# Two-kind attention, then a leaky-ReLU feed-forward layer: the start of the schedule laid out anew

## The chip, the cores and the metric

One core of a Trainium2 chip runs the whole program. Five engines share the work: TensorE (PE in the profile) multiplies matrices into PSUM, VectorE (DVE) and ScalarE (ACT) move and transform tiles, GpSimd (POOL) casts, sets constants and issues some of the transfers, SyncE (SP) issues most transfers. The metric is the device time of one execution in microseconds (us), the lower the better. Before the change the median of three runs was 291.47 us (291.08 to 293.45).

## The reference

Four batches, 8 heads, 768 positions, head size 64. Heads 0, 2 and 6 ("retrieval") attend causally to everything before them; the other five ("streaming") see the first 4 positions (the sinks) and a window of the last 64. The attention output, laid out as 3072 rows of 512, goes through two matrix products with a leaky ReLU between them.

```python
scores = scale * np.matmul(q, k.transpose(0, 1, 3, 2))
stream_keep = causal & (is_sink | in_win)
scores = np.where(mask[None, :, :, :], scores, -1000000000.0)
a = np.exp(scores - np.max(scores, axis=-1, keepdims=True))
a = a / (np.sum(a, axis=-1, keepdims=True) + 1e-09)
x = np.matmul(a, v)            # then rows (batch, position) by 512
h = x @ w_in                   # 512 -> 2048
g = np.maximum(0.01 * h, h)
out = g @ w_out                # 2048 -> 512
```

## The kernel before

The 3072 rows are cut into eight **chunks** of 384 rows, two per batch (even chunks are a batch's first half, `c == 0`; odd ones, `c == 1`, also attend to the first half). For each chunk n the work is:

- **load** (L68): q, k and v come from memory as three fp32 tiles named `f`, of which the pool holds 4. For chunks 0 and 1, k and q are one transfer each (chunk 0's are halves); a later tile is three transfers of 256 KB. Chunks 0 and 1 are issued on SP, chunk 2 on POOL, the others on SP.
- **casts** to bf16 by POOL (`cast_qk`, `cast_v`, L183 to L192): k to `kb`, q to `qb`, v to `va`. Chunk 0 is cast by DVE, ACT and POOL together.
- **v_shift** (L194): the streaming heads read v at an offset of 64 rows; two transfers issued on ACT copy `va` to `vb`. For chunk 0 this is done with matmuls by a shift matrix (`v_shift_pe`, L201).
- **prep_pair** (L215): for a pair of heads, 3 transposes of `kb` and 3 of `qb` on PE, then three moves out of PSUM, two into `kt` and one into `qt`. The PSUM tag `pt` has a single bank, so the next pair's transposes wait until the three moves are done. Four pairs a chunk.
- **attention** (class `Attention`): units of a head. A unit has a score part (`qk`: matmuls into a PSUM bank `psS`, an exponential on ACT into `at` or `ats`, a mask on DVE) and a value part (`do_av`: matmuls by `va`/`vb` into `po`). A retrieval head has 2 units in an even chunk and 5 in an odd one, a streaming head 1. The sink unit (L269) serves all streaming heads. `finish` normalizes a pair of heads on DVE into `xs`; `x_t` transposes `xs` on PE and ACT moves it to `xt`. `slots` (L379) lays the units out so that a unit's values come two slots after its scores.
- **product 1** (`in_slots`, L415): 16 ticks of 4 matmuls, each followed by the leaky ReLU on ACT into `g`.
- **product 2** (`out_slots`, L427): three PSUM results of 16 matmuls each, cut into 16 slots of 2 to 4 matmuls; `py` has one bank; DVE copies a result to `o` and SP stores it.

The whole order is written out by hand: `run` emits lists of slots, `merge(a, b)` spreads list b evenly between the entries of list a, and every engine executes its instructions in the order emitted. From chunk 2 on a loop does the same for each n: product 1 of chunk n, product 2 of chunk n - 1 and the attention of chunk n + 1 (with the preps of chunk n + 2 between) are merged.

The stretch ahead of this loop, the **ramp**, is laid out by itself (L471 to L541): chunk 0's first four heads are scored, its v is cast and shifted, their values begin, and then the second half of its q and k is cast; weights are issued on POOL (`w_in` four times, then `w_out` four times, then chunk 2). Then come chunk 1's attention merged with half of product 1 of chunk 0, the rest of product 1 of chunks 0 and 1 alone, product 2 of chunk 0 alone, nine slots of product 2 of chunk 1 merged with the preps and the attention of chunk 2, and the preps of chunk 3 alone. The loop starts with seven slots of product 2 of chunk 1 left.

Of the kernel before, what the change touches and what calls it, by code (L numbers as in the profile page):

```python
# [17 lines left out]
CH = 384  # L18
# [3 lines left out]
def kernel(  # L22
# [72 lines left out]
    load(0, "k", 0)  # L95
    load(0, "q", 0)
    load(0, "v")
    load(0, "k", 1)
    load(0, "q", 1)
# [18 lines left out]
    ats = [bf(f"ats{i}", 3, 4, 64) for i in range(4)]  # L118
# [7 lines left out]
    def zeros(i):  # L126
        eng = nc.vector if i == 0 else nc.gpsimd
        eng.memset(kt[i][64:128, :, 0, :], 0.0)
        eng.memset(kt[i][0:64, :, 1, :], 0.0)
        nc.gpsimd.memset(va[i][:, :, :, D], 1.0)  # L130
        nc.gpsimd.memset(ksink[i][:], 0.0)
        nc.gpsimd.memset(vs[i][:, 0, :], 0.0)

    def constants():
# [10 lines left out]
        for a in ats:  # L145
            nc.gpsimd.memset(a[:, :, 1:3, :], 0.0)
# [47 lines left out]
    def v_shift(n):  # L194
# [3 lines left out]
        nc.scalar.dma_start(out=vb[i][0:64, lo:hi], in_=va[i][64:128, lo:hi])  # L198
        nc.scalar.dma_start(out=vb[i][64:128, lo:hi], in_=va[i][0:64, lo + 1 : hi + 1])

    def v_shift_pe():  # L201

        for t in range(2):
# [8 lines left out]
            nc.scalar.activation(out=vb[0][:, t, 1:8:2, :], in_=src, func=ACTF.Copy)  # L212
            nc.scalar.activation(out=vb[0][:, t, 4, :], in_=p[:, 4 * w : 5 * w], func=ACTF.Copy)
# [32 lines left out]
    class Attention:  # L246
        def __init__(self, n, score_tags=("psS",)):
# [5 lines left out]
            self.tags = score_tags  # L253
            self.sc = 0
# [3 lines left out]
        def av(self, p, hh, qi, lhsT, rhs):  # L258
            first = p not in self.po
            if first:  # L260
                self.po[p] = bank("po", [128, 3, 2, D + 1], FP32)
# [7 lines left out]
        def sink(self):  # L269
            i, c = self.i, self.c  # L270
            if c == 0:
                for h in range(H):
                    if not IS_RETR[h]:
# [3 lines left out]
                s = self.score()  # L277
                nc.tensor.matmul(s[:, 0 : 7 * (D + 1)], lhsT=e_sink[:], rhs=va[i][:, 0, 1:H, :],
                                 start=True, stop=True)
                nc.vector.tensor_tensor(  # L280
                    vs[i][:, 1:H, :], s[:, 0 : 7 * (D + 1)].rearrange("p (h d) -> p h d", h=7),
                    m_sink[:, 1:H, :], op=ALU.mult)
# [8 lines left out]
        def retr(self, h):  # L291
# [5 lines left out]
            for grp in groups:  # L297
                box = {}

                def qk(grp=grp, box=box):  # L300
                    s = self.score()
                    a = rot.tile([128, CH], BF16, name="at", tag="at", bufs=5)
# [76 lines left out]
        def slots(self, extra=()):  # L379
# [7 lines left out]
            last = {p: max([j for j, u in enumerate(units) if u[2] == p]) for p in range(4)}  # L387
            last[0] = max(last[0], [j for j, u in enumerate(units) if u[1] is None][0])
# [83 lines left out]
    ktb, qtb = cast_tile("k", 0), cast_tile("q", 0)  # L472

    def cast_half(half):
        hs = slice(4 * half, 4 * half + 4)
        nc.vector.tensor_copy(ktb[:, :, hs], qk_src("k", 0)[:, :, hs])
        nc.scalar.activation(out=qtb[:, :, hs], in_=qk_src("q", 0)[:, :, hs], func=ACTF.Copy)

    a0 = Attention(0, ("psS", "ph"))
    cast_half(0)  # L480
    prep_pair(0, 0, "pt", "vva")
    prep_pair(0, 1, "py", "aav")
    u = [a0.units[h] for h in range(H)]
    first = u[0] + u[2]
    run([x[0] for x in first])
    nc.gpsimd.tensor_copy(va[0][:, 0, :, 0:D], v_src(0)[:, 0])
    nc.vector.tensor_copy(va[0][:, 1, :, 0:D], v_src(0)[:, 1])
    nc.gpsimd.tensor_copy(va[0][:, 2, :, 0:D], v_src(0)[:, 2])
    late_constants()
    run([x[0] for x in u[1] + u[3]])  # L490
    sink_mask()
    cast_qk(1)
# [100 lines left out]
```

## Time and profile before

| what | value |
|---|---|
| median of three runs | 291.47 us (291.08 to 293.45) |
| the profiled execution: its own time | 291.4 us |
| its span, first to last instruction | 289.7 us |
| mean granted clock of PE | 0.971 |
| busy PE, ACT, DVE, POOL | 250.7, 142.7, 114.9, 67.3 us |
| moved by DMA | 32.11 MB (27.26 MB read from memory, 6.29 MB written) |

The page shows busy times of the engines, a picture of the span in 40 slices, the DMA queues, the chain of work that ended last and the costliest groups. In a row of a timeline stand the start, the length, the engine, the line, the operation and, in brackets, how long the engine had been idle and what released it. In a row of stretches stand its bounds, its length and, for each engine, busy time and count, then the granted PE clock (1.00 is full), the share of the 16 DMA engines that was busy and GB/s. Matmuls are pipelined: the step from one start to the next is shorter than the duration that a row shows; the chain rows give the steps.

### The profile page before, as it was taken

The page shows a single profiled execution, that of the slowest core. Times are in us where ns is not written, and L with a number is a line of the kernel's source. Part 1 is how long each engine was busy: PE and PEld are TensorE (multiplying, and loading weights), DVE is VectorE, ACT ScalarE, POOL GpSimd, SP SyncE. Part 2 cuts the span into 40 slices and gives each one's busy share as a digit, 9 for nine tenths or more (in the row PEclk, how much of TensorE's full clock was granted, in tenths as well). Part 3 has the DMA queues.
Part 4 walks back from the last instruction along what each step waited for, and adds up shares of the span by engine and source line. Part 5 has one row for each costly group of instructions (what it writes and reads, how often), then busy time and mean ns, then how long its engine had stood idle before and what let it go on. Part 6 is the DMA issues. An engine that isn't in the chain of part 4 may idle for free.

```text
span 289.7 us, 5396 instructions
## 1 busy us (share of the span) xinstructions
PE 250.7 (87%) x2164; PEld 153.4 (53%) x2164; DVE 114.9 (40%) x320; ACT 142.7 (49%) x311; POOL 67.3 (23%) x113
## 2 busy tenths in 40 slices
PE   0658469899976756999989999999999999999995
PEld 0447336555434433666556656666566566655544
DVE  6757324200046744255455523554455124311012
ACT  2644747667002511776545466654554657643310
POOL 7579326920004243520042004300000000000000
PEclk9999978999999985999999999999999999999999
DMA  8999999500239799910793079502000301010022
GB/s 188 252 214 194 188 226 239 121 0 0 75 113 224 152 222 204 221 47 3 158 207 85 27 147 195 116 36 75 36 7 33 94 37 38 0 38 36 36 74 73
DMA packets 66921, 32.11 MB, mean 111 GB/s; under 512 B 54032, under 2 KB 62480, under 8 KB 66896
## 3 DMA queue, kind: packets, MB, share of 16 engines
q1 hardware_dynamic: 60832, 22.81, 35.6%
q0 software_dynamic: 4944, 6.55, 12.6%
q10 hardware_dynamic: 1120, 2.40, 3.6%
q8 instruction: 17, 0.28, 0.4%
q14 instruction: 8, 0.07, 0.1%
HBM read 27.26 MB, written 6.29 MB: 116 GB/s over the span
## 4 chain that ended last, share of the span: by engine, by line
PE 77%; DVE 11%; ACT 5%; DMA 4%; issue 2%; ACTq 0%
PE ph L421 29%; PE py L434 23%; PE po L263 6%; PE pt L223 4%; PE psS L306 4%; DVE kt L233 3%; PE psS L434 3%; DMA vb<-va 3%; PE pt L376 2%; DVE xs L370 2%; PE psS L341 2%; ACT ats L346 1%; DVE qt L233 1%; PE psS L286 1%; DMA f<-in_k_dram 1%
## 5 line engine op out<-in xcount | busy, mean ns | idle before, releaser
L421 PE MATMUL ph<-xt,w_in_bf 128*128 128x384 bf16 x512 | 103.6, 331 | 0.0
L423 ACT ACTIVATE g<-ph 128x384 bf16<-128x384 f32 x128 | 62.8, 491 | 64.9 <-PE ph L421 62.9
L434 PE MATMUL py<-w_out_bf,g 128*128 128x512 bf16 (+1 forms) x336 | 87.2, 375 | 0.3
L421 PEld LDWEIGHTS <-w_in_bf 128*128 128x128 bf16 x512 | 46.4, 99 | 29.4 <-issue 3.4
L311 ACT ACTIVATE at<-psS 128x384 bf16<-128x384 f32 x81 | 38.7, 490 | 31.4 <-PE psS L306 30.5
L434 PEld LDWEIGHTS <-g 128*128 128x128 bf16 x400 | 36.3, 98 | 28.7 <-issue 2.5
L439 DVE COPY o<-py 128x512 f32<-128x512 f32 (+1 forms) x21 | 14.2, 677 | 56.6 <-PE py L434 56.6
L315 DVE TENSOR_TENSOR at<-at,m_caus 128x128 bf16<-128x128 bf16 x72 | 16.7, 261 | 42.1 <-ACT at L311 41.9
L187 POOL CAST kb<-f 128x512 bf16<-128x512 f32 x21 | 13.0, 626 | 78.2 <-DMA f<-in_k_dram 78.2
L306 PE MATMUL psS<-qt,kt 128*128 128x384 bf16 (+2 forms) x105 | 27.8, 309 | 3.3 <-ACT at L311 3.3
L233 DVE COPY kt<-pt 64x384 bf16<-64x384 bf16 x54 | 20.3, 377 | 19.1 <-PE pt L223 18.5
L263 PE MATMUL po<-va,at 128*128 128x65 bf16 x252 | 22.5, 201 | 0.7 <-DVE at L315 0.5
L223 PE MATMUL pt<-ident,kb 128*128 128x128 bf16 x81 | 10.0, 239 | 15.0 <-DVE qt L233 8.1
L263 PEld LDWEIGHTS <-at 128*128 128x128 bf16 x252 | 17.0, 103 | 9.4 <-issue 4.4
L350 DVE TENSOR_TENSOR ats<-ats,m_win 128x384 bf16<-128x384 bf16 x40 | 15.0, 377 | 17.1 <-ACT ats L346 16.7
L346 ACT ACTIVATE ats<-psS 128x384 bf16<-128x384 f32 x37 | 17.9, 491 | 4.9 <-PE psS L341 4.8
L377 ACT ACTIVATE xt<-pt 128x384 bf16<-128x384 bf16 x30 | 14.6, 488 | 9.2 <-PE pt L376 8.7
L223 PEld LDWEIGHTS <-kb 128*128 128x128 bf16 x96 | 8.0, 108 | 20.5 <-DVE qt L233 8.4
L370 DVE TENSOR_TENSOR xs<-po,linv 128x384 bf16<-128x384 f32 x32 | 17.8, 557 | 1.1
L263 PEld LDWEIGHTS <-ats 128*128 128x128 bf16 x240 | 12.4, 102 | 6.5 <-issue 2.8
L376 PE MATMUL pt<-ident,xs 128*128 128x128 bf16 x90 | 10.4, 226 | 6.1 <-DVE xs L370 5.0
L341 PEld LDWEIGHTS <-kt 128*128 128x128 bf16 x240 | 12.8, 103 | 5.3 <-issue 0.5
(87 smaller groups left out, 234.3 us busy)
## 6 DMA issues: line engine op xcount, KB each, us to landing
out_dram<-o SPq DMA_DIRECT2D x23, 256.0 KB, 2.0
f<-in_v_dram SPq DMA_DIRECT2D x21, 256.0 KB, 5.0
f<-in_k_dram SPq DMA_DIRECT2D x15, 256.0 KB, 4.8
f<-in_q_dram SPq DMA_DIRECT2D x15, 256.0 KB, 5.1
w_in_bf<-in_moe_w_in_dram POOLq DMA_DIRECT2D x4, 512.0 KB, 9.0
w_out_bf<-in_moe_w_out_dram POOLq DMA_DIRECT2D x4, 512.0 KB, 16.5
vb<-va ACTq DMA_DIRECT2D x8, 195.0 KB, 5.6
vb<-va ACTq DMA_DIRECT2D x6, 130.0 KB, 3.2
```

Of the source, the lines that this page charges most:

```text
L223: nc.tensor.transpose(pt[:, e, g, :], cast[nm, n][:, g, 2 * p : 2 * p + 2, :], ident[:])
L233: nc.vector.tensor_copy(dst, src)
L263: nc.tensor.matmul(o, lhsT=lhsT, rhs=rhs, start=first, stop=False, skip_group_check=True)
L306: nc.tensor.matmul(s[:, off : off + w], lhsT=kt[i][:, p, hh, 128 * kj : 128 * kj + 128], rhs=qts[n][:, p, lo:CH], start=(j == 0), stop=(j ...
L311: nc.scalar.activation(out=a[:, 0:off], in_=s[:, 0:off], func=ACTF.Exp, scale=SM)
L315: nc.vector.tensor_mul(a[:, off : off + 128], a[:, off : off + 128], m_caus[:])
L341: nc.tensor.matmul(s[:, 64 * m : 64 * m + 64], lhsT=kt[i][:, p, hh, k0 : k0 + 128], rhs=qts[n][:, p, 64 * m : 64 * m + 64], start=(m == 0) ...
L346: nc.scalar.activation(out=av_, in_=s[:, 0:CH].rearrange("p (j e f) -> p j e f", j=3, e=2), func=ACTF.Exp, scale=SM)
L370: nc.vector.tensor_tensor(xs[:], po[:, :, :, 0:D], linv.to_broadcast([128, 3, 2, D]), op=ALU.mult)
L421: nc.tensor.matmul(ph[:, 0:CH], lhsT=w_in_bf[:, g, 128 * t : 128 * t + 128], rhs=xts[n][:, g, :], start=(g == 0), stop=(g == KG - 1))
L423: nc.scalar.activation(out=gs[n][:, t, :], in_=ph[:, 0:CH], func=ACTF.Prelu, alpha=0.01)
L434: nc.tensor.matmul(py[n][:, 0 : c1 - c0], lhsT=gs[n][:, ng, 128 * tt : 128 * tt + 128], rhs=w_out_bf[:, ng, c0:c1], start=(ng == 0), stop= ...
```

## The change

It rewrites the ramp; the loop from chunk 2 on and its helpers stay. Seen by engine queue:

- **SP**: both halves of k and q of chunk 0 are issued ahead of its v. The pool of `f` tiles grows from 4 to 5. The two `v_shift` transfers of chunks 1 and 2 move from ACT to SP.
- **POOL**: chunk 2 is issued between `w_in` and `w_out`. Chunk 3's nine loads are issued on POOL (before: SP), k and q ahead of chunk 2's v cast. The two memsets of the second `kt` go to DVE.
- **PE, chunk 0**: all four pairs are prepared, and heads 0 to 3 and the sinks scored, ahead of the first value matmul; heads 4 to 7 are scored between values. `at` goes from 5 to 6 buffers, `ats` from 4 to 5. The values of chunk 0's shift leave PSUM half by ACT, half by DVE.
- **chunk 1**: its heads run in the order 0, 2, 6, 1, 3, 4, 5, 7, the pair 6/7 accumulates in `py`, and all 16 ticks of product 1 of chunk 0 are merged in.
- **chunk 2**: its preps and attention are merged with product 1 of chunk 1 (before: with nine slots of product 2 of chunk 1).
- **chunk 3**: its preps are merged with product 2 of chunk 0. The loop starts with all 16 slots of product 2 of chunk 1 left.

POOL's queue from the weights to the casts of chunk 2 (`w_in_bf`, `w_out_bf` are the weights, `f` a staged load, `kt_92`, `va_94` the second set of k and v). Before:

```order
L90 DMA w_in_bf<-in_moe_w_in_dram 128x4x512 x4
L192 CAST va_93<-f 128x8x64 x3
L93 DMA w_out_bf<-in_moe_w_out_dram 128x4x512 x4
L77 DMA f<-in_k_dram 128x8x64 x3
L77 DMA f<-in_q_dram 128x8x64 x3
L77 DMA f<-in_v_dram 128x8x64 x3
L128 MEMSET kt_92 64x4x768
L129 MEMSET kt_92 64x4x768
```

and with the change:

```order
L90 DMA w_in_bf<-in_moe_w_in_dram 128x4x512 x4
L189 CAST va_93<-f 128x8x64 x3
L77 DMA f<-in_k_dram 128x8x64 x3
L77 DMA f<-in_q_dram 128x8x64 x3
L77 DMA f<-in_v_dram 128x8x64 x3
L93 DMA w_out_bf<-in_moe_w_out_dram 128x4x512 x4
L129 MEMSET va_94 128x48
L130 MEMSET ksink_100 128x512
L131 MEMSET vs_98 128x65
L184 CAST kb<-f 128x512 x3
L184 CAST qb<-f 128x512 x3
L77 DMA f<-in_k_dram 128x8x64 x3
```

Chunk 2 moved past the four `w_out` transfers, the `kt_92` memsets left, and six loads of chunk 3 stand between the casts of chunk 2's q and v.

ACT's queue where chunk 2's attention begins (`g` is the leaky ReLU of product 1, `at` and `ats` exponentials). Before:

```order
L423 ACTIVATE g<-ph 128x384 x25
L198 DMA vb_96<-va_94 64x1040
L199 DMA vb_96<-va_94 64x1040
L311 ACTIVATE at<-psS 128x384 x2
L346 ACTIVATE ats_103<-psS 128x3x2x64
L289 ACTIVATE at_sink<-psS 128x256
```

and with the change:

```order
L433 ACTIVATE g<-ph 128x384 x4
L319 ACTIVATE at<-psS 128x384
L433 ACTIVATE g<-ph 128x384
L319 ACTIVATE at<-psS 128x384
L433 ACTIVATE g<-ph 128x384
L354 ACTIVATE ats_101<-psS 128x3x2x64
L433 ACTIVATE g<-ph 128x384
L297 ACTIVATE at_sink<-psS 128x256
```

Where 25 leaky ReLUs stood in a row, exponentials of chunk 2 now alternate with those of product 1.

DVE's queue at the same place, from the last normalization of chunk 1 with the change:

```order
L376 RECIPROCAL linv<-py 128x6
L378 TENSOR_TENSOR xs<-py,linv 128x384
L127 MEMSET kt_92 64x4x384
L128 MEMSET kt_92 64x4x384
L235 COPY kt_92<-pt 64x384 x2
L235 COPY qt<-pt 128x384
```

The two memsets stand on DVE between chunk 1's last normalization and the first move of chunk 2's preps; before, three copies of product 2's results stood there.

The diff, cut to its core:

```diff
@@ load, first loads
-            stage[nm, n] = rot.tile([128, 3 * H * D], FP32, name="f", tag="f", bufs=4)
+            stage[nm, n] = rot.tile([128, 3 * H * D], FP32, name="f", tag="f", bufs=5)
-    load(0, "k", 0)
-    load(0, "q", 0)
+    for half in range(2):
+        load(0, "k", half)
+        load(0, "q", half)
     load(0, "v")
-    load(0, "k", 1)
-    load(0, "q", 1)
     load_chunk(1)
-    ats = [bf(f"ats{i}", 3, 4, 64) for i in range(4)]
+    ats = [bf(f"ats{i}", 3, 4, 64) for i in range(5)]
@@ zeros, v_shift
-        eng = nc.vector if i == 0 else nc.gpsimd
+        eng = nc.vector
-    def v_shift(n):
+    def v_shift(n, eng=None):
+        eng = eng or nc.scalar
@@ Attention.slots
-        def slots(self, extra=()):
+        def slots(self, extra=(), order=range(H)):
...
-            for h in range(H):
-                if h == 2:
+            for h in order:
+                if seen == {0, 1} or (2 in seen and h == 1):
                     units.append((self.sink, None, None))
+                seen.add(h)
                 units += self.units[h]
@@ the ramp
+    nc.vector.tensor_copy(ktb[:, :, lo], k0[:, :, lo])
+    nc.scalar.activation(out=qtb[:, :, lo], in_=q0[:, :, lo], func=ACTF.Copy)
+    nc.gpsimd.tensor_copy(ktb[:, :, hi], k0[:, :, hi])
+    late_constants()
     prep_pair(0, 0, "pt", "vva")
     prep_pair(0, 1, "py", "aav")
...
+    qk(*R0)
+    nc.scalar.activation(out=qtb[:, :, hi], in_=q0[:, :, hi], func=ACTF.Copy)
+    qk(*S1)
+    prep_pair(0, 2, "po", "vva")
+    prep_pair(0, 3, "po", "aav")
...
     cast_v(1)
+    load_chunk(2, nc.gpsimd)
     for i in range(4):
         load_w("out", i)
-    load_chunk(2, nc.gpsimd)
+    v_shift(1, nc.sync)
+    qk(*R2)
+    nc.vector.tensor_copy(va[0][:, 1, :, 0:D], v0[:, 1])
+    qk(*S3)
+    a0.sink(values=False)
     v_shift_pe()
+    a0.sink_values()
+    av(*R0)
+    qk(*S4)
+    av(*S1)
     xs0 = a0.finish(0)
+    qk(*S5)
+    av(*R2)
...
-    v_shift(1)
-    a1 = Attention(1).slots()
-    in0, in1 = in_slots(0), in_slots(1)
-    run(a1[0:8], merge(in0[0:8], a1[8:]))
+    a1 = Attention(1, po_tags=("po", "po", "po", "py")).slots(order=[0, 2, 6, 1, 3, 4, 5, 7])
+    run(a1[0:6], merge(in_slots(0), a1[6:]))
     zeros(1)
-    run(in1[0:8], in0[8:12], in1[8:12], in0[12:16], in1[12:16])
-    run(out_slots(0, ("py", "ph", "py")))
     cast_qk(2)
+    load(3, "k", eng=nc.gpsimd)
+    load(3, "q", eng=nc.gpsimd)
     cast_v(2)
-    v_shift(2)
-    load_chunk(3)
-    out1 = out_slots(1)
+    load(3, "v", eng=nc.gpsimd)
+    v_shift(2, nc.sync)
     a2 = preps(2) + Attention(2).slots()
-    run(merge(out1[0:9], a2))
+    run(merge(in_slots(1), a2))
     cast_qk(3)
     cast_v(3)
-    v_shift(3)
     load_chunk(4)
-    run(preps(3))
-    outs = out1[9:]
+    run(merge(out_slots(0), preps(3)))
+    v_shift(3)
+    outs = out_slots(1)
```

More of the change, by code (lines that the diff above doesn't have):

```diff
@@ L144, in constants @@
         nc.gpsimd.memset(e_sink[:], 0.0)
-        for a in ats:
-            nc.gpsimd.memset(a[:, :, 1:3, :], 0.0)
     def late_constants():
@@ L246, with __init__ @@
     class Attention:
-        def __init__(self, n, score_tags=("psS",)):
+        def __init__(self, n, score_tags=("psS",), po_tags=("po", "po", "po", "po")):
             self.n = n
@@ L260, in av @@
             if first:
-                self.po[p] = bank("po", [128, 3, 2, D + 1], FP32)
+                self.po[p] = bank(self.po_tags[p], [128, 3, 2, D + 1], FP32)
             o = self.po[p][:, qi, :, :] if hh is None else self.po[p][:, qi, hh, :]
@@ L267, in score, with sink_values, sink @@
             return bank(self.tags[self.sc % len(self.tags)], [128, 512], FP32)
-        def sink(self):
+        def sink_values(self):
+            i = self.i
+            s = self.score()
+            nc.tensor.matmul(s[:, 0 : 7 * (D + 1)], lhsT=e_sink[:], rhs=va[i][:, 0, 1:H, :],
+                             start=True, stop=True)
+            nc.vector.tensor_tensor(
+                vs[i][:, 1:H, :], s[:, 0 : 7 * (D + 1)].rearrange("p (h d) -> p h d", h=7),
+                m_sink[:, 1:H, :], op=ALU.mult)
+        def sink(self, values=True):
             i, c = self.i, self.c
@@ L276, in sink @@
                         nc.vector.tensor_copy(ksink[i][r, p, NS * h : NS * h + NS], kt[i][r, p, hh, 0:NS])
[L277 to L282, printed above, removed]
+                if values:
+                    self.sink_values()
             s = self.score()
```

76 lines of the change are left out of this document (39 added, 37 removed).

## The prediction

> **What bounds the kernel now.** I read the page's picture of the span first, then the stretches of the ramp, then who waited for whom in its worst stretch.
>
> ```profile
> PE   0658469899976756999989999999999999999995
> PEclk9999978999999985999999999999999999999999
> ```
>
> Of the stretches (bounds, length, busy time of PE, its weight loads, DVE, ACT and POOL, then clock, DMA share, GB/s):
>
> ```profile
> 33.00:37.00 4.00, 2.45 (x24) 1.86 (x24) 1.14 (x4) 3.78 (x9) 0.88 (x1) 0.75 1.16 174
> 37.00:41.00 4.00, 1.58 (x12) 0.68 (x10) 0.36 (x1) 0.97 (x2) 0.88 (x1) 0.83 1.18 246
> 41.00:45.00 4.00, 4.00 (x33) 2.61 (x33) 1.22 (x5) 2.54 (x6) 1.77 (x2) 0.60 1.24 239
> 55.50:72.76 17.26, 17.26 (x101) 9.58 (x100) 0.00 (x0) 12.23 (x25) 4.37 (x8) 1.00 0.00 0
> 83.10:88.00 4.90, 2.02 (x22) 1.06 (x19) 3.49 (x10) 0.00 (x0) 0.25 (x1) 1.00 0.73 171
> ...
> 100.00:106.00 6.00, 3.72 (x42) 2.14 (x39) 2.70 (x9) 1.93 (x5) 2.09 (x4) 1.00 1.08 220
> 106.00:112.50 6.50, 2.36 (x19) 1.60 (x20) 3.61 (x11) 0.00 (x0) 1.91 (x4) 0.55 1.26 200
> 175.00:190.00 15.00, 15.00 (x154) 9.62 (x152) 6.72 (x19) 9.64 (x21) 5.02 (x8) 1.00 0.70 150
> ```
>
> The first digits are PE's share of 40 slices: from about 118 us on PE is full, so the loop is bound by PE and its work does not change. All there is to win lies ahead of it. Two stretches are thin: 33 to 41, and 83 to 112.5, where chunk 2's attention and the preps of chunks 2 and 3 run beside only nine slots of product 2. Between them, from 55.5 to 72.76, PE runs product 1 alone, full, while DVE does nothing and no byte moves (share 0.00).
>
> ```profile
> POOL kb L187 <- DMA f<-in_k_dram: 34.5, 6, 27.9
> PE pt L223 <- DVE qt L233: 8.1, 7, 1.5
> PE pt L376 <- DVE xs L370: 2.5, 4, 0.9
> ```
>
> These are waits within 83.1 to 112.5 (in total, times, longest). PE waits for DVE's moves and normalizations, chains of small steps with little else to run; POOL waits for chunk 3.
>
> **The steps.** Chain rows give start, length and count:
>
> ```profile
> 113.28 1.28 PE ph L421 x4
> 167.52 0.65 PE ph L421 x4
> 76.21 3.45 PE ph L434 x16
> 139.81 0.65 PE py L434 x3
> 168.17 0.77 PE py L434 x3
> 198.04 0.77 PE py L434 x3
> ```
>
> and from the timeline, the transposes of two prep pairs and what runs between them:
>
> ```profile
> 84.92 0.34 PE L223 MATMUL pt<-ident,kb 128*128 128x128 bf16 x3 [1.47 <-DVE qt L233]
> 85.27 0.81 PE L434 MATMUL py<-w_out_bf,g 128*128 128x512 bf16 x3
> 86.64 0.34 PE L223 MATMUL pt<-ident,kb 128*128 128x128 bf16 x3 [0.56 <-DVE qt L233]
> ```
>
> A tick of product 1 is 0.65, sixteen 10.4; at the half clock it is 1.28. Product 2 is 3 x 3.45 = 10.35. A pair's transposes take 0.35 (84.92 to 85.27), four 1.4. The three rows of product 2 begin loop passes n = 3, 4 and 5. Pass 4 lasts 29.87, so an odd chunk's attention is 29.87 - 10.4 - 10.35 - 1.4 = 7.7; pass 3 lasts 28.36, so an even one is 6.2, both with the waits that the loop leaves. After pass 3 begins, 289.7 - 139.81 = 149.89 remain.
>
> With the change pass 2 has an odd chunk's attention, four preps and all of product 2 of chunk 1, like pass 4: 29.87. So the span is (start of the loop) + 29.87 + 149.89, and I need the start of the loop, stage by stage.
>
> **Chunk 0 and the preps of chunk 1.** Three things move.
>
> ```profile
> 10.54 0.48 ACT L311 ACTIVATE at<-psS 128x384 bf16<-128x384 f32 x1
> ...
> 13.03 1.27 PE L209 MATMUL po<-va,shift 128*128 128x260 bf16 x8 [0.82 <-DVE shift L149]
> 14.36 1.03 PE L263 MATMUL po<-va,at 128*128 128x65 bf16 x12
> 14.73 0.85 ACT L477 ACTIVATE qb<-f 128x768 bf16<-128x768 f32 x1
> 16.17 1.14 DVE L233 COPY kt<-pt 64x384 bf16<-64x384 bf16 x2 [1.03 <-PE pt L223]
> 17.79 0.97 ACT L235 ACTIVATE kt<-py 64x384 bf16<-64x384 bf16 x2
> 19.36 1.26 DVE L276 COPY ksink<-kt 64x4 bf16<-64x4 bf16 x5
> 34.01 2.51 ACT L311 ACTIVATE at<-psS 128x384 bf16<-128x384 f32 x5
> 34.55 0.32 PE L306 MATMUL psS<-qt,kt 128*128 128x384 bf16 x1 [3.30 <-ACT at L311]
> ```
>
> Second halves of q and k ahead of v let all pairs be prepared early. ACT's and DVE's new order from head 0's last exponential (ends at 11.0): q's half 0.85, an exponential 0.5 and its mask 0.5, DVE's `kt` moves 1.1, ACT's three moves 1.5, two exponentials of head 2 1.0, masks and a cast of v on DVE 1.5. So the sink copies start at about 17.9, 1.5 before 19.36. But the shift (1.27) and head 0's values (half of 1.03) now stand behind them: 1.8 later. The rest of chunk 0 is the same work in another order, and its tail is the same chain: each prep pair's three moves, then the exponentials of chunk 1, which start at 34.01 behind the last move. I take 34.3. Bounds: 31.0, if the 3.30 that PE waits there vanished, and 37.6, if as much were added. After five exponentials at 0.5 (2.51 for 5), a score and its values, product 1 starts at 37.1.
>
> The same bytes move: the DMA share is over 1 from 33 to 45 and zero from 55.5 on. `w_out` behind chunk 2 costs nothing, as product 2 of chunk 0 comes last. More buffers of `f`, `at` and `ats` and the split of the shift's copies between ACT and DVE I take at nothing, inside the bounds above. On SP the two `v_shift` pairs now stand ahead of chunk 4's loads and wait for POOL's casts; chunk 4 can then go out from about 52 and is wanted at about 92, and no store is due before. POOL's queue decides when chunk 2 is there:
>
> ```profile
> 19.59 3.14 POOL L90 DMA_DIRECT2D w_in_bf<-in_moe_w_in_dram  x4
> 28.87 0.89 POOL L77 DMA_DIRECT2D f<-in_k_dram  x1 [0.45 <-DMA w_in_bf<-in_moe_w_in_dram]
> 41.22 0.88 POOL L77 DMA_DIRECT2D f<-in_q_dram  x1 [2.88 <-DMA w_out_bf<-in_moe_w_out_dram]
> 47.80 0.88 POOL L77 DMA_DIRECT2D f<-in_v_dram  x1 [0.65 <-DMA f<-in_k_dram]
> 54.80 1.72 POOL L187 CAST kb<-f 128x512 bf16<-128x512 f32 x3
> ```
>
> The ninth and later issues each wait until the one eight before has landed: the ninth load of chunk 2, the 17th issue, at 47.80 for the ninth. From the second weight (28.87) to the sixth (41.22) they land 3.1 apart; chunk 2's nine land from 47.80 to about 55, some 1 apart. With `w_in` landed by about 31, chunk 2 follows to about 42 and `w_out` to about 54. POOL waits for chunk 2's own k and q until about 37, casts them by 42, and then the loads of chunk 3's q hold its queue until half of `w_out` has landed: chunk 2's values are cast by about 52. All these are estimates from the rows above. Even cast last of all, as now (k at 54.80, then q and v at 1.7 each, to 60), the values are needed only at about 65. So the load is off the path.
>
> **Product 1 of chunk 0 with chunk 1's attention.** 10.4 + 7.7 x 19/25 (19 of 25 slots are left) = 16.3. ACT has 16 leaky ReLUs and 19 other operations at 0.5, 17.5, under the sum below. The half clock of 33 to 45 now, after PE had stood idle, comes again once: about 4 us at half speed, 2.0. Chunk 1's last normalization leaves a tail (waits of up to 0.9 per `xs`, above), 1.3. Sum 19.6, end at 56.7. Bounds -3.3 (no half clock, no tail) and +2.0 (twice the half clock). The wait for `vb` that holds PE now disappears, as the streaming heads come last:
>
> ```profile
> 40.91 0.19 PE L263 MATMUL po<-vb,ats 128*128 128x65 bf16 x1 [2.42 <-DMA vb<-va]
> ```
>
> On the clock the trace has 0.55 in 106 to 112.5, with PE busy 2.36 of 6.5 and no wait over 1.5. The Trainium skill ("TensorE: Matmul & The Clock Gate", Part 1, on the HAM clock gate) says that the clock is either half or full, goes to half after an idle window of some 3.4 us and to full after as long of sustained work. By that rule the stretch at half would cost 1.7 in place of 2.0 and the sum be 0.3 less. The trace disagrees on the way down: here the clock fell without an idle gap of that length.
>
> **Product 1 of chunk 1 with chunk 2.** 10.4 + 1.4 + 6.2 = 18.0. The four preps share one bank: their period is 1.72 (84.92 to 86.64), and one prep and one tick fill 1.0, so three gaps of 0.7, 2.2. Ahead of the first move DVE now clears `kt_92`:
>
> ```profile
> 1.18 1.34 DVE L128 MEMSET kt<- 64x1536 uint32 x1 [1.18 <-PEq L574]
> 83.15 0.69 DVE L439 COPY o<-py 128x512 f32<-128x512 f32 x1 [2.76 <-PE py L434]
> ```
>
> Two of 1.34 are 2.7, covered by two ticks (1.3); 1.4 remain, and chunk 2's moves queue behind. Sum 21.6, end at 78.3. Bounds: 18.0, and today's loss. From 83.1 to 106 nine slots of product 2 (27 matmuls, 5.8), four preps and the even attention, 13.4 of work, took 22.9, a loss of 9.5 against my 3.6: +5.9. I stay near the low one since 16 ticks cover more than nine slots and in the loop the same attention is covered.
>
> **Product 2 of chunk 0 with the preps of chunk 3.** 10.35 + 1.4, and three times `py` passes through DVE's copy (0.69 and some 0.2 on either side, 0.9): 2.7. Sum 14.4, loop at 92.7. Bounds -2.7 and +1.5. Now the loop starts at 112.5, but with 21 matmuls (4.5) of product 2 left; then it has 48.
>
> **Sum.** 92.7 + 29.9 + 149.9 = 272.5; the profiled execution is 291.4 for a span of 289.7, so 1.7 more: **274.2 us**, 17.2 less than the profiled run and 17.3 less than the median of 291.47.
>
> **Rivals.**
> 1. *Chunk 2's chains stay exposed.* They lose as much inside product 1 as now: 274.2 + 5.9 = 280.1. For it: the gaps between preps are one tick, and ACT shares its queue among ReLUs and exponentials. Against: the loop. Chance 0.22.
> 2. *The ramp is better covered.* Chunk 0's tail gives up the 3.3 of waiting and chunk 2 adds only its 18.0: 274.2 - 3.3 - 3.6 = 267.3. For it: one wait fewer on `vb`, more buffers. Against: the moves of the preps keep their order. 0.17.
> 3. *Slower: the half clock holds.* If PE's gaps among preps and moves keep the clock at half through both stages after 56.7, their 29.8 of full-speed work take 29.8 more, while the 6.3 of other losses vanish beneath: 297.7. It decides where 17 us more of such work than of vanished loss are at half. For it: 106 to 112.5 at 0.55, by preps alone. Against: 83 to 88, as thin, kept 1.00, and ticks fill most gaps now. 0.04. By the rule of the Trainium skill above this could not happen, as no idle gap is so long; the row of 106 is why it keeps its chance.
> 4. *Chunk 2 arrives late.* POOL's chunk-3 issues hold the values 4 us past need: 278. 0.03. That nothing is gained, as the transfers were the bound after all: the zero share of 55.5 to 72.76 speaks against; 291, 0.01.
>
> The forecast has 0.53. About 1% is what a measurement of this kernel can tell from no change. Faster by more takes the forecast, 1, 2 and 4's late arrival: 0.95; slower is 3, 0.04; the same 0.01. The bounds add up to 261 and 287 if all fall one way; 8 in 10 I put between 267.0 and 281.5, which takes in rivals 1 and 2.
>
> **What would show it.**
>
> ```profile
> 43.07 0.49 ACT L423 ACTIVATE g<-ph 128x384 bf16<-128x384 f32 x1 [0.74 <-PE ph L421]
> ```
>
> This is the first leaky ReLU now. Right: it comes at about 38.5; product 1 of chunk 0 ended near 57; exponentials of chunk 2 from about 63 between ReLUs; the loop's full PE from about 93; no idle stretch beside it. Wrong: the start of chunk 1's exponentials off 34.3 by over 3; PE waiting for a cast or `vb` of chunk 2; a clock under 1.00 after 60; gaps at the preps of chunk 2 over 0.7 or waits of several us on `xs`.

## The result and the profile after

The changed kernel takes **275.39 us** (median of 4 runs, 274.26 to 275.83), beside 291.33 (291.08 to 293.45) for the kernel before: a ratio of 0.943, 95% interval 0.938 to 0.949. In the last group of experiments, on another chip than the groups before it, it took 274.76 beside 291.63, 0.944 (0.939 to 0.948). The forecast was 274.2, in a range of 267.0 to 281.5. The profiled execution took 275.26 for a span of 273.6. One kernel among the experiments, the new chunk 0 with the old stages, has times in two groups 6 us apart, so it is read by the places in its trace and not by its total.

The picture of the span on the page of the changed kernel, in the same 40 slices:

```profile
PE   1647498857897899999999999999999999999995
PEclk9999889999999999999999999999999999999999
```

PE is full from the 15th slice on, at about 96 us, where the kernel before got there at about 118; in place of the two thin stretches (33 to 41 and 83 to 112.5) there is one, at 55 to 68 us (the digits 5 and 7), and the clock reads under full in the 5th and 6th slice alone. The stretches (same columns as before: bounds, length, busy time of PE, its weight loads, DVE, ACT, POOL, clock, DMA share, GB/s):

```profile
33.00:37.00 4.00, 4.00 (x29) 2.34 (x28) 0.59 (x3) 2.83 (x7) 2.21 (x3) 0.60 1.06 234
37.00:41.00 4.00, 4.00 (x40) 2.63 (x39) 0.59 (x3) 3.88 (x10) 2.64 (x6) 1.00 1.03 215
41.00:45.00 4.00, 2.94 (x27) 1.77 (x26) 2.93 (x2) 2.90 (x7) 4.00 (x9) 1.00 1.13 209
...
55.00:60.00 5.00, 2.84 (x24) 1.47 (x22) 3.67 (x9) 1.07 (x3) 3.56 (x5) 1.00 1.04 224
60.00:65.00 5.00, 3.56 (x34) 2.21 (x33) 3.33 (x12) 3.16 (x7) 1.85 (x3) 1.00 1.10 218
```

From 33 us on, half clock is left in 33 to 37 alone. From 55 to 65, where PE once ran product 1 alone and full, it is now busy 6.4 of 10 us and DVE 7.0: there the preps of chunk 2 stand. In return the stretch from 83 to 112.5 of the kernel before is gone. The timeline gives the start of each stage (start, duration, instruction, and in brackets the engine's idle time ahead of it and what ended it):

```profile
31.89 3.57 ACT L319 ACTIVATE at<-psS 128x384 bf16<-128x384 f32 x7
32.43 0.32 PE L314 MATMUL psS<-qt,kt 128*128 128x384 bf16 x1 [3.83 <-ACT at L319]
34.90 1.46 PE L431 MATMUL ph<-xt,w_in_bf 128*128 128x384 bf16 x4
36.40 0.49 ACT L433 ACTIVATE g<-ph 128x384 bf16<-128x384 f32 x1 [0.94 <-PE ph L431]
36.45 0.81 PE L431 MATMUL ph<-xt,w_in_bf 128*128 128x384 bf16 x4
54.49 0.33 PE L225 MATMUL pt<-ident,kb 128*128 128x128 bf16 x3
57.24 0.34 PE L225 MATMUL pt<-ident,kb 128*128 128x128 bf16 x3 [1.60 <-DVE qt L235]
58.96 0.34 PE L225 MATMUL pt<-ident,kb 128*128 128x128 bf16 x3 [0.56 <-DVE qt L235]
60.69 0.34 PE L225 MATMUL pt<-ident,kb 128*128 128x128 bf16 x3 [0.58 <-DVE qt L235]
78.75 2.11 PE L444 MATMUL py<-w_out_bf,g 128*128 128x512 bf16 x9
83.48 1.46 PE L444 MATMUL py<-w_out_bf,g 128*128 128x512 bf16 x6 [0.78 <-DVE o L449]
88.21 0.81 PE L444 MATMUL py<-w_out_bf,g 128*128 128x512 bf16 x3 [0.78 <-DVE o L449]
93.85 0.81 PE L444 MATMUL py<-w_out_bf,g 128*128 128x512 bf16 x3 [1.35 <-DVE o L449]
```

| place | forecast | measured |
|---|---|---|
| first exponential of chunk 1 | 34.3 | 31.89 |
| product 1 of chunk 0 begins | 37.1 | 34.90 |
| first leaky ReLU | 38.5 | 36.40 |
| the stage of product 1 of chunk 0, with chunk 1's attention | 19.6, to 56.7 | 19.6, to 54.49 |
| product 1 of chunk 1, with chunk 2 | 21.6, to 78.3 | 24.3, to 78.75 |
| product 2 of chunk 0, with chunk 3's preps | 14.4, to 92.7 | 15.1, to 93.85 |
| from there to the end of the span | 179.8 | 273.6 - 93.85 = 179.75 |

The sum came out 1.1 low at the loop, but as 2.2 too much in front and 3.4 too little behind. The waits of PE from 34 to 95 us (total, times, longest) tell what the stages lost:

```profile
PE py L444 <- DVE o L449: 2.9, 3, 1.4
PE pt L225 <- DVE qt L235: 2.7, 3, 1.6
PE pt L384 <- DVE xs L378: 1.6, 4, 0.6
PE psS L294 <- DVE ksink L288: 1.4, 2, 0.9
PE py L266 <- DVE at L323: 1.1, 1, 1.1
PE pt L384 <- ACT xt L385: 0.8, 1, 0.8
```

All but the last, 9.7 of 10.5, end with DVE. The wait for `at`, whose masks DVE makes, was not in the sum. Its place in the timeline, with what POOL did meanwhile:

```profile
39.11 0.36 DVE L323 TENSOR_TENSOR at<-at,m_caus 128x128 bf16<-128x128 bf16 x2 [0.68 <-ACT at L319]
41.68 1.73 POOL L184 CAST kb<-f 128x512 bf16<-128x512 f32 x3
42.07 3.21 DVE L323 TENSOR_TENSOR at<-at,m_caus 128x128 bf16<-128x128 bf16 x3 [2.60 <-ACT at L319]
43.35 1.72 POOL L184 CAST qb<-f 128x512 bf16<-128x512 f32 x3
44.65 0.27 PE L266 MATMUL py<-va,at 128*128 128x65 bf16 x3 [1.06 <-DVE at L323]
```

Two masks of chunk 1 take 0.36 at 39.11; three of the same kind take 3.21 at 42.07, and end just after POOL's six casts of chunk 2, which run from 41.68 to 45.07 without a gap.

### The profile page after: what moved, and what is told of

Its sections match the earlier page's. It is cut to its first block, busy times and chain, and to the rows that moved or that the text cites. A ratio compares the mean times of both kernels' runs of the same rounds, so it can differ in the third digit from the quotient of the medians.

```text
span 273.6 us, 5398 instructions
## 1 busy us (share of the span) xinstructions
PE 240.9 (88%) x2164; PEld 148.4 (54%) x2164; DVE 119.5 (44%) x323; ACT 142.0 (52%) x309; POOL 70.8 (26%) x122
## 4 chain that ended last, share of the span: by engine, by line
PE 75%; DVE 13%; ACT 7%; issue 2%; DMA 2%; SPq 0%; ACTq 0%; DVEq 0%
PE py L444 27%; PE ph L431 25%; PE po L266 6%; PE psS L314 4%; PE pt L225 3%; PE psS L444 3%; DVE kt L235 3%; DVE ats L358 2%; DVE at L323 2%; DVE xs L378 2%; ACT at L319 2%; PE pt L384 2%; PE psS L349 2%; DMA f<-in_q_dram 2%; ACT ats L354 1%
## 5 line engine op out<-in xcount | busy, mean ns | idle before, releaser
L431 PE MATMUL ph<-xt,w_in_bf 128*128 128x384 bf16 x512 | 104.7, 327 | 0.0
L444 PE MATMUL py<-w_out_bf,g 128*128 128x512 bf16 (+1 forms) x352 | 91.2, 374 | 3.2 <-DVE o L449 2.9
L431 PEld LDWEIGHTS <-w_in_bf 128*128 128x128 bf16 x512 | 44.9, 98 | 24.7 <-issue 0.3
L319 ACT ACTIVATE at<-psS 128x384 bf16<-128x384 f32 x81 | 39.2, 489 | 13.2 <-PE psS L314 12.7
L323 DVE TENSOR_TENSOR at<-at,m_caus 128x128 bf16<-128x128 bf16 x72 | 20.1, 310 | 47.2 <-ACT at L319 46.9
L314 PE MATMUL psS<-qt,kt 128*128 128x384 bf16 (+2 forms) x104 | 27.3, 301 | 3.8 <-ACT at L319 3.8
L184 POOL CAST kb<-f 128x512 bf16<-128x512 f32 x21 | 12.7, 622 | 65.9 <-DMA f<-in_k_dram 65.7
L449 DVE COPY o<-py 128x512 f32<-128x512 f32 (+1 forms) x22 | 14.9, 678 | 32.6 <-PE py L444 32.6
L358 DVE TENSOR_TENSOR ats<-ats,m_win 128x384 bf16<-128x384 bf16 x40 | 15.7, 393 | 19.3 <-ACT ats L354 19.1
L266 PE MATMUL po<-va,at 128*128 128x65 bf16 x237 | 20.5, 199 | 0.0
L225 PE MATMUL pt<-ident,kb 128*128 128x128 bf16 x81 | 9.1, 222 | 8.6 <-DVE kb L495 5.2
L225 PEld LDWEIGHTS <-kb 128*128 128x128 bf16 x96 | 7.9, 103 | 14.4 <-DVE kb L495 5.2
L349 PEld LDWEIGHTS <-kt 128*128 128x128 bf16 x240 | 12.7, 102 | 5.4
L184 POOL CAST qb<-f 128x512 bf16<-128x512 f32 x21 | 12.7, 615 | 10.1 <-DMA f<-in_q_dram 7.0
L189 POOL CAST va<-f 128x512 bf16<-128x512 f32 x21 | 13.0, 635 | 8.3 <-DMA f<-in_v_dram 8.2
```

The lines of the kernel that those rows point to most:

```text
L184: nc.gpsimd.tensor_copy(tb[:, g], src[:, g])
L225: nc.tensor.transpose(pt[:, e, g, :], cast[nm, n][:, g, 2 * p : 2 * p + 2, :], ident[:])
L266: nc.tensor.matmul(o, lhsT=lhsT, rhs=rhs, start=first, stop=False, skip_group_check=True)
L314: nc.tensor.matmul(s[:, off : off + w], lhsT=kt[i][:, p, hh, 128 * kj : 128 * kj + 128], rhs=qts[n][:, p, lo:CH], start=(j == 0), stop=(j ...
L319: nc.scalar.activation(out=a[:, 0:off], in_=s[:, 0:off], func=ACTF.Exp, scale=SM)
L323: nc.vector.tensor_mul(a[:, off : off + 128], a[:, off : off + 128], m_caus[:])
```

## Experiments: where the gain is

The theory: the gain is the pairing of the stages (chunk 1's and chunk 2's chains beside product 1, product 2 of chunk 0 beside preps). Its rivals: the transfers, or chunk 0's new order with the clock behind it. In each of the diffs the lines are of the kernel named.

**The old chunk 0 with the new stages.** The changed kernel with the part from the first load to the last prep of chunk 1 as before, but chunk 2 ahead of `w_out`:

```
-    for half in range(2):
-        load(0, "k", half)
-        load(0, "q", half)
+    load(0, "k", 0)
+    load(0, "q", 0)
     load(0, "v")
+    load(0, "k", 1)
+    load(0, "q", 1)
...
-    v_shift(1, nc.sync)
...
+    v_shift(1)
     a1 = Attention(1, po_tags=("po", "po", "po", "py")).slots(order=[0, 2, 6, 1, 3, 4, 5, 7])
```

> The chunk 0 of before (loads, casts, order, shift copies, v_shift of chunk 1 on ACT after its preps) with chunk 2 loaded ahead of w_out, and from there the stages of the changed kernel. Theory (the pairing of the stages is most of the gain): 277 to 280, the 275.4 of the changed kernel plus the 2.1 by which chunk 1's first exponential comes later and up to 2.4 for vb and the clock. Rival (chunk 0's new order and the clock): 286 or above. If the two halves add up, the gains of this run and of the one with the new chunk 0 alone sum to 16 us.

Measured: 278.55 us (277.12 to 278.86) beside 291.20, ratio 0.957 (0.950 to 0.963). So 12.7 of the 16 are there without the new chunk 0; the other 3 are what that is worth on top. Product 1 begins at 37.59 in this trace, 2.7 after the 34.90 of the changed kernel. The run changes all the stages at once. By the places in the two traces (with the nine ticks that the kernel before leaves for later added at 0.65 each, and its 27 matmuls of product 2 taken off at 0.216 each) some 2.9 of it fall in chunk 1's stage, which also gets its new order of heads, 6.6 between there and the loop, and 3.5 behind the start of the loop, less 0.4 by which chunk 1's scores come later; no run takes these apart.

**The new chunk 0 with the old stages.** The other half alone:

```
-    a1 = Attention(1, po_tags=("po", "po", "po", "py")).slots(order=[0, 2, 6, 1, 3, 4, 5, 7])
-    run(a1[0:6], merge(in_slots(0), a1[6:]))
+    a1 = Attention(1).slots()
+    in0, in1 = in_slots(0), in_slots(1)
+    run(a1[0:8], merge(in0[0:8], a1[8:]))
...
+    run(out_slots(0, ("py", "ph", "py")))
+    cast_qk(2)
```

> The changed kernel's chunk 0, loads and v_shift of chunk 1 up to the last prep of chunk 1, and from there the stages of before: heads in order, the two products 1 and product 2 of chunk 0 alone, then nine slots of product 2 of chunk 1 beside chunk 2, then the preps of chunk 3. Theory (most of the gain is in the pairing of the stages): 4 to 5 us faster than before, 286 to 288, 2.1 from the first exponential of chunk 1 at 31.9 in place of 34.0, the rest from the wait of 2.4 on vb that an earlier v_shift takes away and from less time at half clock. Rival (chunk 0's new order and the clock behind it are the gain): 280 or less.

> The new chunk 0 with the old stages once more, as its four times lay apart (one at 286.0, three at 292.9 to 294.5). Theory (the new chunk 0 gains some 4 to 5 in front, of which a mask held 3.9 by POOL's casts takes most back): 286 to 290. Rival (chunk 0 is the gain): 280 or less. Rival (without the new stages the early chunk 2 gives back all of it): 291 or above.

Measured: two of ten runs took 285.95 and 286.23, the other eight 291.94 to 295.34 (medians 293.26 and 292.57, beside 291.20 and 291.63). The rival with 280 or less is out. Whether this half gains 5 or nothing is not settled, as neither of the two short runs left a trace. The traces of two of the other eight show a loss in chunk 1's stage; this is the second:

```profile
46.61 4.53 DVE L323 TENSOR_TENSOR at<-at,m_caus 128x128 bf16<-128x128 bf16 x2 [0.16 <-ACT at L319]
```

Chunk 1's last masks stand beside POOL's casts of chunk 2 (47.11 on), PE waits 3.9 for them, and product 2 of chunk 0 begins at 74.27, where the kernel before, whose chunk 1 starts 2 us later, begins it at 72.59. Behind the wait the clock is 0.50 until about 57, and the 100 matmuls of product 1 from 54.55 on take 19.89 where they take 17.48 in the kernel before.

**The load order alone, in the kernel before.**

```
     cast_v(1)
+    load_chunk(2, nc.gpsimd)
     for i in range(4):
         load_w("out", i)
-    load_chunk(2, nc.gpsimd)
```

> The kernel before with one edit: the nine loads of chunk 2 are issued ahead of the four of w_out. Theory (the gain is in what runs beside what, not in the transfers): within 1 us of before, 290.5 to 292.5, because chunk 2's preps still stand after product 2 of chunk 0, at 83 us; chunk 2's k is then cast some 8 us before the 54.8 of now, and nobody wants it. Rival (the transfers were what held the ramp): 5 us or more faster, 286 or less. A third way: w_out comes too late for product 2 of chunk 0 at 76 us; it can only be so if it lands after 76, some 20 us after the last byte of now, and then the time is above 292.5.

Measured: 298.44 us (296.87 to 298.84), ratio 1.025 (1.018 to 1.032). Neither the theory (no change) nor the first rival: it is 7.2 slower, and not by the third way either, as product 2 of chunk 0 waits for no byte. It begins 6.8 later, at 79.36. Two waits of PE in the stretch before it have grown:

```profile
PE po L263 <- DMA vb<-va: 6.6, 1, 6.6
PE po L263 <- DVE at L315: 3.4, 2, 3.1
```

In the kernel before these are 2.4 and 0.5. The second of the two copies of `vb`, issued after chunk 1's preps, now lands 11.3 after its issue (32.67 to 44.00), in the kernel before 7.4 (33.36 to 40.77). I take it that it meets more bytes on the way, since chunk 2 and `w_out` now go out by 40.84 instead of 47.80; the next run bears this out only in that an earlier issue ends the wait. And POOL, free sooner, casts chunk 2 at 47.70 to 52.8, beside chunk 1's masks (three of them 4.48 from 48.36), where before it cast from 54.80 on, nearly all of it after DVE's last work of the stage. 4.2 and 2.9 make 7.1.

**The same, with the wait for `vb` taken away.** `v_shift(1)` from ACT's queue after the preps to SP's right behind the loads:

```
+    v_shift(1, nc.sync)
     v_shift_pe()
...
-    v_shift(1)
     a1 = Attention(1).slots()
```

> The kernel before with chunk 2 loaded ahead of w_out, as in the run that took 298.44, and besides v_shift of chunk 1 issued on SP right behind the loads, in place of on ACT after chunk 1's preps. Theory (that run lost 7.2 to two things: 4.2 more of waiting for vb, whose copies stood behind the bytes of chunk 2 and w_out, and 3.1 for a mask held by POOL's casts, which now fall into chunk 1's attention): with the wait for vb gone (6.6), 291 to 293, still no faster than before. Rival (early loads gain on their own once vb is out of the way): 288 or less. Rival (the loss has another cause): 296 or above.

Measured: 295.01 us (293.83 to 295.85), ratio 1.012 (1.006 to 1.018). The wait for `vb` is gone and the kernel is still slower than before, so the rival, a gain by early loads alone, falls. But 3.4 came back where the theory had 6.6, so the expectation failed in size. Three masks now meet the casts of k, q and v and take 5.2 us; PE waits 4.6 for masks in all, and in the next stretch its clock is half. Product 2 of chunk 0 begins at 75.64, 3.0 after the 72.59 of the kernel before.

```profile
48.47 5.20 DVE L316 TENSOR_TENSOR at<-at,m_caus 128x128 bf16<-128x128 bf16 x3 [1.41 <-ACT at L312]
48.52 1.72 POOL L187 CAST kb<-f 128x512 bf16<-128x512 f32 x3
50.19 1.72 POOL L187 CAST qb<-f 128x512 bf16<-128x512 f32 x3
51.87 1.73 POOL L192 CAST va<-f 128x512 bf16<-128x512 f32 x3
52.61 0.27 PE L264 MATMUL po<-va,at 128*128 128x65 bf16 x3 [3.79 <-DVE at L316]
```
```profile
55.00:60.00 5.00, 4.12 (x23) 2.31 (x22) 0.75 (x2) 1.60 (x4) 0.00 (x0) 0.52 0.05 9
```

**The load order alone, undone in the changed kernel.**

```
     cast_v(1)
-    load_chunk(2, nc.gpsimd)
     for i in range(4):
         load_w("out", i)
+    load_chunk(2, nc.gpsimd)
```

> The changed kernel with the loads of w_out put back ahead of those of chunk 2, and nothing else. Theory (the load order is off the path): 274.5 to 277. Chunk 2's k and q are then cast from about 49 to 52.5 us, its values from about 55; its first prep stands at 54.5, its values are wanted at about 65. The slow masks at 42.07 (3.21 for three) become 0.6, as no cast runs beside them then. Rival (the early load is what lets chunk 2 stand beside product 1): PE waits for a cast of chunk 2 at 54 to 60, by 4 us or more, 279 or above.

Measured: 275.41 us (274.19 to 276.48), ratio 0.947 (0.939 to 0.955): the time of the changed kernel. Chunk 2's k is cast at 47.29 and its q done at 52.0, ahead of the first prep at 54.4, and no wait of PE for a cast is in the list. The masks of chunk 1 are quick again (0.59 for three from 42.96), but three of chunk 2 are held now, beside casts of chunk 3:

```profile
62.13 2.31 DVE L323 TENSOR_TENSOR at<-at,m_caus 128x128 bf16<-128x128 bf16 x3
64.36 1.32 DVE L358 TENSOR_TENSOR ats<-ats,m_win 128x384 bf16<-128x384 bf16 x1
```

PE waits 0.5 for those masks and 1.4 behind them for the sink copies, so a hold in one place came in place of a hold in another. The early load is not what lets chunk 2 stand beside product 1. Of the three theories the pairing stands.

## Experiments: what the stages lost

Four edits of the changed kernel, each against one of the waits above, and all together. The changed kernel did not run beside the four single edits; its 275.39 (274.26 to 275.83) is from the first measurement. So a gain of 1 or 2 us in the total is no more than the spread, and what each edit does is read from the waits in its trace.

**Second key buffer cleared early.** DVE's two clears go ahead of product 1 of chunk 0:

```
-    run(a1[0:6], merge(in_slots(0), a1[6:]))
+    run(a1[0:6])
+    zeros_kt(1)        # the two DVE memsets of zeros(1)
+    run(merge(in_slots(0), a1[6:]))
```

> The changed kernel with DVE's two clears of the second key buffer (2 of 1.34 us) put ahead of product 1 of chunk 0, where DVE has nothing from about 34.8 to 38.2 us, instead of ahead of chunk 2's first prep. Theory (the clears hold the first prep, as the prediction's term of 1.4 had it): the first two preps of chunk 2 stand 1.7 apart in place of 2.75, and all that follows comes 1.0 earlier: 274.4 where the changed kernel has 275.4. Rival (stage 2 is bound by the chain of moves and exponentials behind them, and the 1.0 is lost to the next wait): 275.4, with longer waits at chunk 2's sink scores.

Measured: 274.62 us (273.25 to 275.24), ratio 0.939 (0.935 to 0.943). The first two preps stand at 55.62 and 57.32, 1.70 apart, with a wait of 0.56 for 1.60. That is the 1.0 of the theory; the total is 0.8 lower, with times that overlap those of the changed kernel.

**Two banks for chunk 2's preps.**

```
-    a2 = preps(2) + Attention(2).slots()
+    a2 = preps(2, ("pt", "py")) + Attention(2).slots()
```

> The changed kernel with chunk 2's four preps in two PSUM banks by turns (pt, py) in place of one. Theory (the preps' period of 1.72 is the bank going round through DVE's three moves): the three gaps of 0.6 to 1.6 that PE waits for DVE's qt shrink to 0.2 or less each, and the last prep comes about 1.6 earlier: 273.8. Rival (DVE's 1.1 per prep behind its clears is the pace, so the waits only move from the preps to the first scores): 275.0 to 275.5.

Measured: 272.78 us (272.08 to 273.50), ratio 0.934 (0.930 to 0.939), more than expected. One wait of 0.62 is left of three, and DVE does one prep behind the other, 1.03 each:

```profile
57.37 0.71 DVE L235 COPY kt<-py 64x384 bf16<-64x384 bf16 x2
58.12 0.36 DVE L235 COPY qt<-py 128x384 bf16<-128x384 bf16 x1
58.39 0.73 DVE L235 COPY kt<-pt 64x384 bf16<-64x384 bf16 x2
```

The last prep is done 1.8 sooner, and behind it the wait for the sink copies is 0.4 in place of 1.4. The stage takes 54.76 to 75.82, 21.1 for 24.3.

**Three bank turns for product 2 of chunk 0.**

```
-    run(merge(out_slots(0), preps(3)))
+    run(merge(out_slots(0, ("py", "po", "po")), preps(3)))
```

> The changed kernel with the three parts of product 2 of chunk 0 in the banks py, po, po, in place of py three times. Theory (three handovers of py through DVE's copy cost 0.78, 0.78 and 1.35): these waits go to zero and the full loop begins 2.9 earlier: 272.5. Rival (the preps of chunk 3 set the length of that stage: four times the transposes, three moves and the way back, or PE waits for them instead): 274.5 to 275.4.

Measured: 272.25 us (271.60 to 273.19), ratio 0.932 (0.928 to 0.936). The second part follows the first without a wait:

```profile
82.53 1.46 PE L444 MATMUL po<-w_out_bf,g 128*128 128x512 bf16 x6
```

No wait for `o` is left, and the stage runs from 78.74 to 90.44, 11.7 where it took 15.1: 10.35 of product 2 and the four preps' 1.4.

**Chunk 2's casts apart.** Behind each of the six casts of k and q comes the issue of one load of chunk 3:

```
-    cast_qk(2)
-    load(3, "k", eng=nc.gpsimd)
-    load(3, "q", eng=nc.gpsimd)
+    for nm in "kq":
+        cast_load(2, nm)   # for g in range(3): the cast of slice g, then the load of slice g of chunk 3
```

> The changed kernel with POOL's six casts of chunk 2's k and q no longer back to back: after each cast comes the issue of one load of chunk 3 (0.88), which POOL has to do anyway. Theory (a DVE mask, two inputs in SBUF, is held while POOL's casts follow one another without a gap, and let in at the first gap): the three masks at 42.07 take 0.6 to 1.8 in place of 3.21, PE's wait there (1.06) goes, 274.4. Rival (the masks are slow for another reason, a late exponential or the DMA traffic): they stay at about 3.2 and the time at 275.4; or the casts' later end (about 50.4 for 45.1) delays chunk 2's first prep: 276 or above.

Measured: 273.74 us (273.38 to 275.31), ratio 0.938 (0.934 to 0.942). The same three masks, among the same casts with a gap behind each:

```profile
41.96 0.62 POOL L193 CAST kb<-f 128x512 bf16<-128x512 f32 x1
41.98 0.72 DVE L333 TENSOR_TENSOR at<-at,m_caus 128x128 bf16<-128x128 bf16 x1 [2.60 <-ACT at L329]
42.52 0.90 POOL L194 DMA_DIRECT2D f<-in_k_dram  x1
42.88 1.24 DVE L333 TENSOR_TENSOR at<-at,m_caus 128x128 bf16<-128x128 bf16 x2 [0.18 <-ACT at L329]
43.41 0.62 POOL L193 CAST kb<-f 128x512 bf16<-128x512 f32 x1
```

They take 1.96 in all for 3.21, the wait of PE for them is gone, and the casts end at 49.8, still ahead of the first prep at 53.6. A wait of 0.4 for a streaming mask, also beside a cast, comes instead. The total is 1.7 lower, more than the 1.1 of the wait, and its times overlap those of the changed kernel. The rival, DMA traffic or a late exponential, falls, as far as one run shows: the bytes and the exponentials are the same.

**All four, and the changed kernel beside them.**

> The changed kernel with all four edits together: second key buffer cleared early, chunk 2's preps in two banks, product 2 of chunk 0 in three bank turns, chunk 2's casts apart. Theory (four separate losses, each on the path): the single gains add up, 275.4 - 0.8 - 2.6 - 3.1 - 1.7 = 267.2. Rival (two of them are the same loss seen twice, or a next wait comes up behind them): 269 or above.

> The changed kernel itself, beside the others on this chip, as the mark for the run with all four edits: 275.4 by every theory; 274.3 to 276.

Measured: 267.91 us (267.23 to 269.38), ratio 0.920 (0.915 to 0.925), beside 274.76 (274.26 to 276.16) for the changed kernel: 6.9 less. That is 0.7 above the sum; the four single gains add up to 8.2, so side by side 1.3 are missing, and the losses are separate for the most part. What PE waits for between 34 and 95 us falls from 10.5 to 2.9:

```profile
PE pt L397 <- DVE xs L391: 1.1, 3, 0.6
PE pt L397 <- ACT xt L398: 0.8, 1, 0.8
PE psS L307 <- DVE ksink L301: 0.8, 1, 0.8
PE pt L238 <- DVE qt L248: 0.2, 1, 0.2
```

## Why the prediction was right, and where not

**What bounds, and where the gain is: right.** The loop ran as forecast to its end (179.75 for 179.8), pass 2 like pass 4 (29.9, from 93.85 to 123.76). Most was won ahead of the loop, as said, but not all: pass 2 of the kernel before took 27.3 with 21 matmuls of product 2, the changed one 29.9 with 48, 5.8 more of work, so some 3.2 of the 16 fall in it. Its first 5.1 us ran at a clock of 0.57 before (112.50 to 117.60) and at 1.00 now. That the load order is off the path was shown in the changed kernel. The prediction had no price for it in the kernel before, nor needed one, but its reason, that the same bytes move, would have missed the 7.2 that it costs there: an early load also sets POOL free, and its casts then hold the masks.

**Chunk 0: 2.4 too late at chunk 1's first exponential.** The step that failed is "the rest of chunk 0 is the same work in another order". One piece of it got shorter. The first cast of k, in the kernel before:

```profile
4.29 2.31 DVE L476 CAST kb<-f 128x768 bf16<-128x768 f32 x1
4.56 1.50 POOL L146 MEMSET ats<- 128x384 bf16 x4
```

and in the changed kernel, where POOL clears `ats` later, at 7.51:

```profile
4.28 0.90 DVE L495 CAST kb<-f 128x768 bf16<-128x768 f32 x1
```

I had read the new place of the `ats` clears as a matter of POOL alone. No run changed it alone; with the old chunk 0 and five clears in that place the cast takes 2.73. But only 0.6 of the 1.4 reach head 0's last exponential, which starts at 9.93 for 10.54, since q's transposes then wait for ACT's cast of q:

```profile
6.38 0.50 PE L225 MATMUL pt<-ident,qb 128*128 128x128 bf16 x3 [0.64 <-ACT qb L496]
9.93 0.48 ACT L319 ACTIVATE at<-psS 128x384 bf16<-128x384 f32 x1
```

From the end of that exponential to the sink copies the sum had 6.9 and it took 6.1 (10.41 to 16.52): 0.8 more. From there to chunk 1's first exponential the sum had 16.4, the 14.65 of the kernel before and 1.8 for the shift and the values; it took 15.4: the last 1.0, whose cause stays open. One thing that the sum lacks stands there: three transposes, which take 0.17 from start to start at full clock, still take 0.32 at 27.65 in the kernel before, while in the changed kernel they take 0.33 at 6.67 and 0.18 from 22.83 on. So PE ran most of chunk 0 at half clock, though the picture's first four slices have a 9 for the clock, and full clock now comes some 5 us sooner. What that is worth no run shows. The wait of 3.8 ahead of chunk 1's scores stayed (3.83 at 32.43, for 3.30), as the forecast had it and rival 2 had not.

**Product 1 of chunk 0: 19.6 for 19.6, by luck.** The half clock was to cost 2.0 (4 us of it). It lasted the 4 us, but from 32.43 on, so that 2.5 of them lie ahead of product 1, and in the stage it cost about 0.6: one tick of 1.27 at 34.90, and from 36.45 on ticks of 0.65. The tail was 0.8 for 1.3 (a wait for ACT's `xt` at 53.58). Against these stand 1.06 of PE's waiting for the held masks, a term that the sum lacked, and 0.8 more of other work (17.1 without waits and half clock, where the sum had 16.3). The casts that hold the masks were forecast to end by 42; they ran until 45.07. The wait for `vb` did vanish, as forecast.

By the Trainium skill ("TensorE: Matmul & The Clock Gate", Part 1, on the HAM clock gate) the clock goes to half after an idle window of some 3.4 us, and full clock comes back after as long of sustained work. The trace agrees here: the idle 3.83 stands ahead of 32.43, half clock follows it, and from 32.43 to the first full tick at 36.45 are 4.0 us.

**Product 1 of chunk 1 with chunk 2: 24.3 for 21.6, the term that was undersized.** The pairing held, and the miss goes the way of rival 1, with 2.7 of its 5.9. Of the preps I had three gaps of 0.7 and 1.4 for the clears, 3.6; PE's waits there are 1.60, 0.56 and 0.58, 2.7 in all, so this term was even too large. What I left out is behind the preps: the scores of the sink wait 1.4 for DVE's copies, and the normalizations of the four pairs 1.6. I had reasoned that "in the loop the same attention is covered"; but in the loop two products stand beside it, here one. A gap over 0.7 at these preps was also among my signs of being wrong, and the first is 1.60: the sign was badly put, as the sum itself has the clears ahead of that prep.

**Product 2 of chunk 0: 15.1 for 14.4.** Three handovers cost 2.9, the term had 2.7; taking them away made the stage 3.4 shorter and the total 3.1. The other 0.5 of the miss I can't place.

**The rivals.** The wait in chunk 0's tail stayed and chunk 2 added more than its 18.0 (rival 2), no half clock after 37 (rival 3), no wait for chunk 2's casts or `vb` (rival 4). That the total came within 1.2 of the forecast is partly luck: 2.2 too much in front and 3.4 too little behind.

## What to carry to other kernels

Ask of each stage which chain of small steps stands beside which long run of matmuls: of the 16 us here 12.7 came with that pairing, and none was lost when the load order was put back. After such a change look again at what the chain's engine does in the new place: a bank that several steps share, a clear put ahead of the first of them, and another engine's work beside them cost 7 more, and each was a change of a few lines. Where a load is made earlier, follow the work that it sets free, and see what that runs beside: earlier loads alone made the kernel 7 slower.

## What the hardware showed beyond expectation

A DVE operation with two inputs in SBUF can be held by POOL for much longer than one POOL instruction. A mask that takes 0.23 us alone took 2.5 in the changed kernel, where six of POOL's casts of 0.57 followed each other without a gap, and 4.2 in the new chunk 0 with the old stages (from 46.96), where nine did; three masks took 3.2, 4.5 and 5.2. With a load's issue (0.9) after each cast three took 2.0. Beside POOL's memsets of the key buffer (42.44 to 47.80 in the kernel before with early loads and `v_shift(1)` on SP) a streaming mask kept its 0.36 (at 44.27), but a causal one took 0.63 beside such a memset in the kernel before (at 52.32). DVE's copies of transposes out of PSUM kept their 0.36 a piece beside casts from chunk 2 on. And the cast of k from SBUF took 2.31 for 0.90 beside memsets.

The Trainium skill ("SBUF — State Buffer", section "SBUF: two separate sides") says that DVE and GpSimd share one pair of ports as an exclusive lock, held for the whole instruction by whichever starts first, and that a DVE operation with two SBUF inputs contends only with a GpSimd operation that reads SBUF. The quick mask beside a memset and the slow ones beside casts agree with that, the one of 0.63 beside a memset does not. The measurement goes further: by the rule a mask would wait for the cast under way, 0.57 at most, and it waited for several. The page's other case, a DVE operation in a two-port mode, which contends with any GpSimd operation, would fit the slow cast of k beside memsets; no run here shows which mode that had.

Left open: why the new chunk 0 with the old stages has two groups of times. In its two traces the 100 matmuls behind the wait for the masks take 19.70 and 19.89 for 17.48, so 2.2 and 2.4 of the loss are the half clock that follows the wait; what the short runs do there is not known.
